# Three more heads with P·v in float32, and an earlier frozen start for two experts

## The chip, the cores and the metric

The kernel runs on one core of a Trainium2 chip. The metric is the time of one execution in microseconds (us), in the median over several. All engines of the core work at the same time, each through its own instructions in order: TensorE (matmuls; PE in rows, its weight loads PEld), VectorE (DVE), ScalarE (ACT), GpSimd (POOL) and SyncE (SP), which here only issues transfers (DMA). They wait for one another by semaphores.

## The reference

Attention over 4 batches of 8 heads, 576 positions and head size 64, with a mask by blocks of 64; its output is the input of a dense layer, and that one's output the input of a top-2 mixture of 8 experts:

```python
scores = np.where(block_i >= block_j, q @ k.T / sqrt(D), -1e9)
attn = softmax(scores); x = (attn @ v) as [2304, 512]
x = ((x @ w1) * (x @ w2)) @ w3 @ w_out            # 512 -> 1024 -> 1024 -> 512
noisy = x @ w_gate + log1p(exp(x @ w_noise)) * noise
top2, top2_w = the two largest of 8 and their softmax
out[t] += top2_w * (relu(x[t] @ w1[e]) @ w2[e])   # for both e of each token
```

## The kernel before

Products that need float32 accuracy are made of F32R halves: `split` writes a high half (a cast, on ScalarE) and a low half (source less high half, on VectorE, or on GpSimd with `low="pool"`), and `mm3` multiplies high·high, high·low and low·high in three matmuls (L470 to L472).

The attention (`attention`) takes 32 heads one after the other. Its operations stand in two strings, FIRST for the first ten steps and LATER, in which each letter is a step: `g` makes transposed probabilities `pt` of a group of columns (transposes, then a copy at L657 and a low half at L659), `a` and `b` multiply them by v (`av`, L678), `c` converts a piece of the dense layer's weights, `f` runs a stretch of that layer. The weights come as 64-bit integers' halves into `stg` by SyncE's loads, are unpacked on VectorE (`stf`, L528 to L530) and split into the pieces `pc0` to `pc11`. Heads 0 to 7 multiply P and v as plain float32 (`vz` is v with ones beside it, `pt` has one slot); heads 8 to 31 use high and low halves of P and v (`vv`, L600 and L601), in which P·v has two passes.

The dense layer (`Moe1`) runs over nine chunks of 256 tokens. `ab(c, f)` for f = 0 to 7 makes x·w1 and x·w2 of a slice (the products `m`, copied at L205, multiplied into `at` at L206, split into `gt`), `yout(c, t, part)` makes the chunk's output rows `y` (copied at L222, stored to `yt`). The router of chunk c runs in small ticks beside the next chunk; it counts the tokens of each expert (`run_cnt`) and scatters their numbers into the table `idt`. `x_load` and `x_prep` bring the attention's output into a chunk's x ahead of time (`xab`, `xr`, `xh`).

The mixture works per expert on 640 slots, five tiles of 128 rows: slots 0 to 2 (s = 0) and 3 to 4 (s = 1). `gather` fetches rows of `yt` by the table's ids, `trans` transposes and splits them (`xt`), `ffn1` makes eight `ht` slices, `ffn2(e, i)` makes an output tile `yo`, and a scatter-add puts it into the output (L933). The pieces of the experts' weights are loaded by `load_next` in order of use, 12 in memory at a time; before the dense layer has ended they go through two staging buffers, `xab` and `xr`. Expert 0's first three tiles start early: after chunk 7 has been counted, in chunk 8's last part, `freeze` fixes those slots, so that they hold tokens of counted chunks only, and `start_early` loads their ids (`ids0`) and gathers. The rest of the mixture runs in `phase3`.

Of the kernel before, what the change touches and what calls it, by code (L numbers as in the profile page):

```python
# [62 lines left out]
ZC, NF = 3, 10  # L63
PIECE_PRIO, W_PRIO, MOE_PRIO = -60, -400, -200
# [17 lines left out]
class Moe1:  # L82
# [22 lines left out]
    def setup(self):  # L105
# [13 lines left out]
        self.tr0 = p2.tile([P, E, NSLOT], I32, name="tr0")  # L119
# [8 lines left out]
    def setup_dram(self, step):  # L128
        nc, a, k = self.nc, self.a, self.k
        if step == 0:  # L130
            tab = k.idt.rearrange("(e s) o -> e (s o)", e=E)
            for dst, src in k.slots(tab, self.tr0):
                nc.sync.dma_start(dst, src)
            nc.sync.dma_start(tab[:, CAP:].rearrange("e (t c) -> t e c", c=P), self.tr1.unsqueeze(1).broadcast_to([NOV, E, P]))
            n = CH // P + 1
            dst = k.yt[NT - CH:, :].rearrange("(a p) d -> p a d", p=P)
            nc.sync.dma_start(dst[:, :, DM:], self.z[:, 0:n * E].rearrange("p (a e) -> p a e", a=n))
            for b in range(DM // CH):
                nc.sync.dma_start(dst[:, :, b * CH:(b + 1) * CH], self.z.unsqueeze(1).broadcast_to([P, n, CH]))
        else:  # L140
            n = -(-(NT // P + 1) // 4) * P
            dst = a["out"][(step - 1) * n:min(step * n, NT + P), :].rearrange("(p a) (b d) -> p (a b) d", p=P, d=CH)
            nc.sync.dma_start(dst, self.z.unsqueeze(1).broadcast_to([P, dst.shape[1], CH]))

# [49 lines left out]
    def ab(self, c, f):  # L194
# [13 lines left out]
        self.marks = (*self.k.split((gt[:, 0, :], gt[:, 1, :]), at, low="pool"), v)  # L208
# [40 lines left out]
    def router(self, c):  # L249
# [102 lines left out]
        for t in range(TPC):  # L352
            y = self.ys[c, t]
            v.tensor_tensor(y[:, DM:ROW], oh[0][:, t, :], oh[1][:, t, :], op=OP.add)
            t0 = (c * TPC + t) * P
            nc.sync.dma_start(k.yt[t0:t0 + P, :], y)
# [6 lines left out]
    def steps(self):  # L363
# [21 lines left out]
        for c in range(NCH):  # L385
# [4 lines left out]
            for f in range(8):  # L390
# [12 lines left out]
            if c == NCH - 1:  # L403
                for _ in self.rt:
                    pass
                self.freeze()
# [12 lines left out]
    def freeze(self):  # L419
# [5 lines left out]
        nc.tensor.matmul(pc[:, 0:1], self.tri[:, 1, :], cb[:, 0:1], start=True, stop=True)  # L425
        m = p2.tile([P, 1], F32, name="miss")
        v.tensor_tensor(m, self.room, pc[:, 0:1], op=OP.subtract)
        v.tensor_scalar(m, m, 0.0, float(NA), op0=OP.max, op1=OP.min)
        v.tensor_tensor(self.run_cnt[:, 0:1], self.run_cnt[:, 0:1], m, op=OP.add)
        self.k.start_early()  # L430

    def tail(self):
# [3 lines left out]
        for _ in self.rest:  # L436
            pass
        for _ in self.rt:
            pass
# [11 lines left out]
class Kernel:  # L451
    def __init__(self, tc, a):
        self.tc, self.nc, self.a = tc, tc.nc, a
        self.loaded = 0
        self.x2w = {}

# [77 lines left out]
    def attention(self):  # L534
        tc, nc, a = self.tc, self.nc, self.a
        moe1 = self.moe1
        with tc.tile_pool(name="p1", bufs=1, side="right") as p1, tc.tile_pool(name="stg", bufs=2, side="right") as self.stg, \
# [13 lines left out]
            px = pxs.enter_context(tc.tile_pool(name="px", bufs=1))  # L551
# [43 lines left out]
            def prep_v(h):  # L595
                c = hd[h]
                if h < H:
# [44 lines left out]
            def g_unit(h, g):  # L642
                c = hd[h]
                pb = pbs[h < H and h % 2]
                if g == 0:
                    if h < H:
                        c.pt = px.tile([P, 1, PTW], F32, name="pt", bufs=2)
                    else:
# [9 lines left out]
                if h >= H:  # L658
# [190 lines left out]
    def load_next(self):  # L849
# [11 lines left out]
        if self.early:  # L861
            t = self.moe1.p2b.tile([P, 1024], F32, name="xr" if n % 2 else "xab")
# [3 lines left out]
        self.split((self.pc[i][:, 0, :], self.pc[i][:, 1, :]), t)  # L866
# [4 lines left out]
    def start_early(self):  # L871
# [4 lines left out]
        self.ids0 = self.pa.tile([P, NA], I32, name="ids0")  # L876
        nc.sync.dma_start(self.ids0, self.slots(self.tab, self.ids)[0][0][:, 0, :])
        self.gather(0, 0)

    def idx(self, e, i):  # L880
        ids = self.ids0[:, i:i + 1] if e == 0 and i < NA else self.ids[:, e, i:i + 1]
# [6 lines left out]
    def gather(self, e, s):  # L888
        for i in self.part(s):
            if self.early:  # L890
                t = self.pa.tile([P, ROW], F32, name="xga", bufs=NA)
# [3 lines left out]
            self.nc.gpsimd.indirect_dma_start(out=t, out_offset=None, in_=self.yt, in_offset=self.idx(e, i))  # L895
# [13 lines left out]
    def ffn1(self, e, s):  # L909
        nc, x, n = self.nc, self.xt[e, s], len(self.part(s)) * P  # L910
        hh = self.ht[e, s] = (self.pa if s == 0 else self.pb).tile([P, 2, 8, n], F32R, name=f"ht{s}")
        for f in range(8):
# [5 lines left out]
            nc.scalar.activation(hh[:, 0, f, :], ph, AF.Relu)  # L918
            nc.vector.scalar_tensor_tensor(hh[:, 1, f, :], ph, 0.0, r32(hh[:, 0, f, :]), op0=OP.max, op1=OP.subtract)  # L919

    def ffn2(self, e, i):
# [9 lines left out]
        yo = self.pa.tile([P, DM], F32, name="yo", bufs=2)  # L931
        nc.scalar.activation(yo, po, AF.Copy, scale=self.wv[e, s][:, o:o + 1])  # L932
        nc.gpsimd.indirect_dma_start(out=self.a["out"], out_offset=self.idx(e, i), in_=yo, in_offset=None, compute_op=OP.add)  # L933

    def phase3(self):
        nc = self.nc
        with self.tc.tile_pool(name="pb", bufs=1, reuse_waits="tile") as self.pb:
            for src, dst in self.slots(self.tab, self.ids):
                nc.sync.dma_start(dst, src)
            for _ in range(4):  # L940
                self.load_next()
            self.gather(0, 1)
            self.gather(1, 0)
            self.gather(1, 1)
            for e in range(E):
                if e == 0:
                    self.trans(0, 1)
                else:
                    self.ffn1(e, 0)
                self.ffn1(e, 1)  # L950
                if e + 1 < E:
                    for s in range(2):
                        self.trans(e + 1, s)
# [4 lines left out]
                for i in range(0 if e else NA, NSLOT):  # L958
# [99 lines left out]
```

## Time and profile before

| | |
|---|---|
| median of 3 runs | 1110.45 us (1108.77 to 1111.13) |
| the profiled execution | 1110.5 us, span 1108.6 us |
| TensorE busy | 1050.8 us (95%) |
| VectorE, ScalarE, GpSimd busy | 569.8, 496.6, 310.7 us |
| TensorE's mean granted clock | 0.985 of full speed |

The span is the time from the first to the last instruction of the trace; the profiled execution's own time is 1.9 us above it. An engine's busy time counts its instructions and leaves out waits.

### The profile page before, as it was taken

What the parts mean: (1) busy time and instruction counts of PE and PEld (TensorE: products, weight loads), DVE (VectorE), ACT (ScalarE), POOL (GpSimd) and SP (SyncE); (2) the same over time, 40 slices, a digit from 0 to 9 for tenths busy, and PEclk for the clock granted to TensorE, in tenths of its full rate; (3) what the DMA queues carried; (4) which work ended last, traced back from release to release, by engine and by line L of the source; (5) the groups of instructions that cost most, each with busy time, mean ns of one, the idle gap of its engine ahead of it and who ended that gap; (6) DMA issues with size and microseconds to landing.
All of it is one profiled execution on the core that took longest, in us unless ns stands there. A gap on an engine that the chain in (4) does not pass through costs nothing.

```text
span 1108.6 us, 17533 instructions
## 1 busy us (share of the span) xinstructions
PE 1050.8 (95%) x6588; PEld 940.1 (85%) x6588; DVE 569.8 (51%) x1269; ACT 496.6 (45%) x1180; POOL 310.7 (28%) x315
## 2 busy tenths in 40 slices
PE   5989878999999999999999998999999999999996
PEld 3767776899898989989999787989898989989894
DVE  6988879866675747433346424433333342424120
ACT  5865546666666666422225324433333333333120
POOL 3110313325152342332442335241313222120202
PEclk9999989899999999999999998999999999999999
DMA  9765775335634463413433148453544445351303
GB/s 224 245 200 187 199 193 184 113 92 126 181 96 108 147 163 97 112 45 58 77 56 111 56 131 229 139 148 100 143 105 136 113 125 124 105 114 30 38 10 41
DMA packets 79442, 135.81 MB, mean 122 GB/s; under 512 B 21005, under 2 KB 45813, under 8 KB 79349
## 3 DMA queue, kind: packets, MB, share of 16 engines
q1 hardware_dynamic: 69237, 113.44, 36.0%
q0 software_dynamic: 10112, 21.16, 10.3%
q8 instruction: 54, 0.88, 0.3%
q14 instruction: 39, 0.32, 0.1%
HBM read 103.92 MB, written 30.66 MB: 121 GB/s over the span
## 4 chain that ended last, share of the span: by engine, by line
PE 78%; DMA 8%; DVE 8%; issue 2%; ACT 1%; SPq 1%; POOL 1%; POOLq 0%; DVEq 0%; ACTq 0%
PE ph L470 13%; PE ph L471 12%; PE ph L472 12%; PE m L470 9%; PE m L472 9%; PE m L471 9%; PE tp L653 4%; PE av L678 4%; DMA stg<-in_w_dram 3%; PE sb L623 2%; PE sb L620 2%; PE m L906 1%; DVE pc L465 1%; DVE nm L634 1%; DMA stf<-in_m_dram 1%
## 5 line engine op out<-in xcount | busy, mean ns | idle before, releaser
L470 PE MATMUL m<-xh,pc 128*128 128x256 f32 x576 | 165.7, 291 | 7.7 <-DVE at L206 5.5
L471 PE MATMUL m<-xh,pc 128*128 128x256 f32 x576 | 163.1, 287 | 2.6 <-DVE xh L465 2.6
L472 PE MATMUL m<-xh,pc 128*128 128x256 f32 x576 | 161.1, 286 | 1.4 <-DVE pc L465 1.4
L470 PE MATMUL ph<-xt,pc 128*128 128x256 f32 (+1 forms) x512 | 157.4, 309 | 5.2 <-ACT xt L461 5.2
L471 PE MATMUL ph<-xt,pc 128*128 128x256 f32 (+1 forms) x512 | 157.5, 308 | 0.0
L472 PE MATMUL ph<-xt,pc 128*128 128x256 f32 (+1 forms) x512 | 157.2, 307 | 0.0
L465 DVE TENSOR_TENSOR pc<-stf,pc 128x1024 fp32r<-128x1024 f32 (+1 forms) x96 | 96.4, 1018 | 104.4 <-ACT pc L461 101.1
L919 DVE SCALAR_TENSOR_TENSOR ht<-ph,ht 128x256 fp32r<-128x256 f32 (+1 forms) x128 | 61.8, 489 | 130.8 <-ACT ht L918 130.7
L470 PE MATMUL ph<-pc,ht 128*128 128x512 f32 x320 | 128.0, 401 | 0.0
L471 PE MATMUL ph<-pc,ht 128*128 128x512 f32 x320 | 126.3, 395 | 0.0
L472 PE MATMUL ph<-pc,ht 128*128 128x512 f32 x320 | 126.2, 395 | 0.0
L933 POOL DMA_INDIRECT out_dram<-yo,ids x40 | 65.1, 1626 | 199.4 <-ACT yo L932 106.6
L461 ACT CAST pc<-stf 128x1024 fp32r<-128x1024 f32 (+1 forms) x96 | 82.2, 872 | 83.8 <-DMA stf<-in_m_dram 50.1
L470 PEld LDWEIGHTS m<-xh,pc 128*128 128x128 f32 x576 | 110.3, 192 | 9.9 <-DVE at L206 6.1
L918 ACT ACTIVATE ht<-ph 128x256 fp32r<-128x256 f32 (+1 forms) x128 | 55.3, 437 | 130.7 <-PE ph L472 130.5
L465 POOL TENSOR_TENSOR gt<-at,gt 128x256 fp32r<-128x256 f32 x72 | 59.0, 823 | 194.3 <-ACT gt L461 184.6
L471 PEld LDWEIGHTS m<-xh,pc 128*128 128x128 f32 x576 | 110.0, 192 | 3.3 <-DVE xh L465 2.9
L639 ACT ACTIVATE pb<-sb,nm 128x288 f32<-128x288 f32 (+3 forms) x192 | 93.7, 497 | 41.1 <-DVE nm L637 19.3
L472 PEld LDWEIGHTS m<-xh,pc 128*128 128x128 f32 x576 | 108.8, 192 | 2.0 <-DVE pc L465 1.6
L470 PEld LDWEIGHTS ph<-xt,pc 128*128 128x128 f32 x512 | 96.6, 189 | 6.0 <-ACT xt L461 5.4
L593 POOL TENSOR_TENSOR kl<-qk,hi 128x576 fp32r<-128x576 f32 x32 | 47.8, 1493 | 179.0 <-ACT hi L591 128.1
L471 PEld LDWEIGHTS ph<-xt,pc 128*128 128x128 f32 x512 | 96.8, 189 | 0.4
(156 smaller groups left out, 2224.0 us busy)
## 6 DMA issues: line engine op xcount, KB each, us to landing
stf<-in_m_dram SPq DMA_DIRECT2D x56, 512.0 KB
qk<-in_qk_dram SPq DMA_DIRECT2D x32, 576.0 KB
stg<-in_w_dram SPq DMA_DIRECT2D x32, 512.0 KB
x<-ev SPq DMA_DIRECT2D x32, 288.0 KB
xab<-x SPq DMA_DIRECT2D x20, 256.0 KB
yt<-y SPq DMA_DIRECT2D x18, 260.0 KB
stg<-in_w_out_dram SPq DMA_DIRECT2D x8, 512.0 KB
v<-in_v_dram SPq DMA_DIRECT2D x24, 160.0 KB
```

What stands on the lines that cost most here:

```text
L461: d = nc.scalar.copy(h, src)
L465: return d, eng.tensor_tensor(l, src, r32(h), op=OP.subtract)
L470: nc.tensor.matmul(out, a, c, start=first, stop=False)
L471: nc.tensor.matmul(out, a, d, start=False, stop=False)
L472: nc.tensor.matmul(out, b, c, start=False, stop=last)
L593: nc.gpsimd.tensor_tensor(c.kl, c.qk[:, 1, :], r32(c.hi[:, 1, :]), op=OP.subtract)
L639: nc.scalar.activation(pb[t][:, k0:k0 + src.free_size()], src, AF.Exp, bias=nm, scale=1.0, accum_out=sums[:, h // H, t + n, h % H:h % H + 1])
L653: nc.tensor.transpose(bank[:, n * P:(n + 1) * P], pb[t][:, kt * P:(kt + 1) * P], self.ident)
L678: nc.tensor.matmul(c.av[:, o0:o0 + w], c.vv[:, kt, :], c.pt[:, i, s0:s0 + w], start=(kt == 0 and i == 0), stop=(kt == 4 and i == m - 1))
L918: nc.scalar.activation(hh[:, 0, f, :], ph, AF.Relu)
L919: nc.vector.scalar_tensor_tensor(hh[:, 1, f, :], ph, 0.0, r32(hh[:, 0, f, :]), op0=OP.max, op1=OP.subtract)
L933: nc.gpsimd.indirect_dma_start(out=self.a["out"], out_offset=self.idx(e, i), in_=yo, in_offset=None, compute_op=OP.add)
```

## The change

`HF = 11`: heads 8 to 10 are multiplied like heads 0 to 7, with P as copied from PSUM and v as loaded. The freeze moves from the end of chunk 8's `ab` into chunk 7 (after f = 5, behind the rest of chunk 6's router) and covers experts 0 and 1; the ids of both are loaded after the first output of chunk 7, and their rows gathered after f = 1 of chunk 8, five tiles at once, since `xga` has five buffers. Rows of chunk 7 in `yt` are zeroed beforehand too. The loads of the experts' first pieces come one by one, and a piece is converted only when two are staged and the next is to be loaded, or when `conv_next` is called. Expert 1's first three tiles go through `trans` and `ffn1` before `phase3`. The last expert makes three output tiles ahead of its second `ffn1`; the last tile's scaling is shared by ScalarE and VectorE.

```diff
+HF = 11
@@ load_v, prep_v, the copy into pt
-                if h < H:
-                    c.vv = vz[h % 2]
+                if h < HF:
+                    if h < H:
+                        c.vv = vz[h % 2]
+                    else:
+                        c.vv = p1.tile([P, 5, P], F32, name="vv")
+                        nc.gpsimd.memset(c.vv[:, :, D:], 0.0)
                     nc.sync.dma_start(c.vv[:, :, 0:D], a["v"][h])
                     return
...
-                if h >= H:
+                if h >= HF:
                     nc.vector.tensor_tensor(c.pt[:, 1, base:base + o], src, r32(h_), op=OP.subtract)
@@ Moe1.steps
-                if c == NCH - 1 and f % 2 == 1:
+                if c == NCH - 1 and (f == 1 or f > 2):
+                    if f == 1:
+                        self.k.load_next()
                     self.k.load_next()
-                    self.k.load_next()
+                if c == NCH - 2 and f == 5:
+                    for _ in self.rt:
+                        pass
+                    self.freeze()
+                if c == NCH - 1 and f == 1:
+                    with self.tc.issue_after(self.marks[1].ins):
+                        self.k.gather(0, 0)
+                        self.k.gather(1, 0)
...
+                    if c == NCH - 2 and (t, part) == (0, 0):
+                        self.k.start_early()
+                    elif c == NCH - 1 and (t, part) == (0, 0):
+                        self.k.load_next()
+                    elif c == NCH - 1 and (t, part) in ((0, 1), (1, 0)):
+                        self.k.conv_next()
@@ run
                     for i in range(NA):
                         self.ffn2(0, i)
+                    self.trans(1, 0)
+                    self.ffn1(1, 0)
                     self.moe1.p2s.close()
@@ load_next
         if self.early:
+            if len(self.staged) == 2:
+                self.conv_next()
             t = self.moe1.p2b.tile([P, 1024], F32, name="xr" if n % 2 else "xab")
...
         nc.sync.dma_start(t, src)
-        self.split((self.pc[i][:, 0, :], self.pc[i][:, 1, :]), t)
+        self.staged.append((i, t))
+        if not self.early:
+            self.conv_next()
+
+    def conv_next(self):
+
+        if self.staged:
+            i, t = self.staged.pop(0)
+            with ExitStack() as es:
+                for m in self.marks if self.early else ():
+                    es.enter_context(self.tc.issue_after(m.ins))
+                self.split((self.pc[i][:, 0, :], self.pc[i][:, 1, :]), t)
@@ phase3
-                else:
+                elif e > 1:
                     self.ffn1(e, 0)
+                if e == E - 1:
+                    for i in range(NA):
+                        self.ffn2(e, i)
                 self.ffn1(e, 1)
```

In the rows that follow, a tile's number behind the underscore tells one use of a name from another, and line numbers are those of the kernel in question (the changed one's are higher).

VectorE in the attention, while head 9 is under way, before (`pt` is the low half of P, `stf` and `pc` a piece of the dense layer's weights, `nm` a maximum for the softmax):

```order
L465 TENSOR_TENSOR pc4_71<-stf_1078,pc4_71 128x512
L634 TENSOR_REDUCE nm2_1608<-sb_1604 128x1
L659 TENSOR_TENSOR pt_1559<-tp_1560,pt_1559 128x448
L530 SCALAR_TENSOR_TENSOR stf_1106<-stg_1074,stf_1106 128x512
L659 TENSOR_TENSOR pt_1559<-tp_1567,pt_1559 128x448
L634 TENSOR_REDUCE nm3_1615<-sb_1611 128x1
L465 TENSOR_TENSOR pc4_71<-stf_1106,pc4_71 128x512
L528 TENSOR_SCALAR stf_1114<-stg_1082 128x512
L206 TENSOR_TENSOR at_1653<-at_1653,m_1628 128x256
L206 TENSOR_TENSOR at_1692<-at_1692,m_1667 128x256
L529 SCALAR_TENSOR_TENSOR stf_1114<-stg_1082,stf_1114 128x512
L659 TENSOR_TENSOR pt_1559<-tp_1576,pt_1559 128x512
```

and with the change:

```order
L553 TENSOR_SCALAR stf_1114<-stg_1082 128x512
L663 TENSOR_REDUCE nm0_1580<-sb_1574 128x1
L663 TENSOR_REDUCE nm1_1582<-sb_1574 128x1
L663 TENSOR_REDUCE nm2_1590<-sb_1586 128x1
L554 SCALAR_TENSOR_TENSOR stf_1114<-stg_1082,stf_1114 128x512
L488 TENSOR_TENSOR pc4_71<-stf_1106,pc4_71 128x512
L213 TENSOR_TENSOR at_1634<-at_1634,m_1609 128x256
L663 TENSOR_REDUCE nm3_1597<-sb_1593 128x1
L555 SCALAR_TENSOR_TENSOR stf_1114<-stg_1082,stf_1114 128x512
L488 TENSOR_TENSOR pc5_72<-stf_1114,pc5_72 128x512
```

The subtractions into `pt` are gone, and the unpacking of `stg_1082` stands ahead of the product `at`.

SyncE at the same place, before (`stg` is a piece of weights, `xab` and `xr` the second chunk's x, `qk` and `v` the next heads'):

```order
L162 DMA xab_1659<-x2_61 64x4x256
L574 DMA qk_1557<-in_qk_dram 128x1152
L162 DMA xab_1659<-x2_61 64x4x256 x2
L519 DMA stg_1082<-in_w2_dram 128x2x256
L167 DMA xr_1660<-rs_62 64x4x256 x2
L583 DMA v_1730<-in_v_dram 128x320
L519 DMA stg_1110<-in_w2_dram 128x2x256
L519 DMA stg_1118<-in_w1_dram 128x2x256
```

and with the change:

```order
L609 DMA vv_1543<-in_v_dram 128x5x64
L544 DMA stg_1082<-in_w2_dram 128x2x256
L713 DMA x2_61<-ev_1512 128x576
L169 DMA xab_1640<-x2_61 64x4x256 x2
L599 DMA qk_1546<-in_qk_dram 128x1152
L169 DMA xab_1640<-x2_61 64x4x256
L174 DMA xr_1641<-rs_62 64x4x256
L169 DMA xab_1640<-x2_61 64x4x256
L544 DMA stg_1110<-in_w2_dram 128x2x256
```

The load of `stg_1082` now goes ahead of the second chunk's x.

ScalarE at the end of chunk 8, before (`pc` are casts of expert 0's pieces from the staging buffers `xab` and `xr`, `y` the two output copies of the chunk):

```order
L205 COPY at_7372<-m_7347 128x256
L461 CAST gt_7375<-at_7372 128x256
L461 CAST pc2_69<-xab_7422 128x1024
L461 CAST pc3_70<-xr_7426 128x1024
L205 COPY at_7409<-m_7384 128x256
L461 CAST gt_7412<-at_7409 128x256
L222 COPY y_7472<-m_7447 128x512
L222 COPY y_7499<-m_7474 128x512
L461 CAST yT_7506<-m_7501 128x4x128
```

and with the change:

```order
L484 CAST pc5_72<-xr_7279 128x1024
L212 COPY at_7395<-m_7370 128x256
L484 CAST gt_7398<-at_7395 128x256
L484 CAST pc0_67<-xab_7327 128x1024
L484 CAST pc1_68<-xr_7368 128x1024
L484 CAST pc2_69<-xab_7410 128x1024
L229 COPY y_7441<-m_7412 128x512
L484 CAST pc3_70<-xr_7427 128x1024
L229 COPY y_7472<-m_7445 128x512
L484 CAST yT_7483<-m_7478 128x4x128
L484 CAST xt0_7587<-m_7590 128x4x128
```

Six pieces are cast behind the last `at` copies in place of two, and the second `y` copy stands behind the cast of the last of them, `pc3`.

ScalarE around expert 0's early tiles, before (`ht` is expert 0's or 1's first layer, `yo` an output tile, `xt` the transposed rows of the next):

```order
L461 CAST pc8_75<-stf_7848 128x1024
L932 ACTIVATE yo_7782<-ph_7757,wv0_7611 128x512
L461 CAST pc9_76<-stf_7852 128x1024
L461 CAST pc10_77<-stf_7856 128x1024
L932 ACTIVATE yo_7810<-ph_7785,wv0_7611 128x512
L461 CAST pc11_78<-stf_7860 128x1024
L461 CAST xt1_7878<-m_7881 128x4x128
L461 CAST xt1_7878<-m_7889 128x4x128
L461 CAST xt0_8017<-m_8020 128x4x128
L932 ACTIVATE yo_7838<-ph_7813,wv0_7611 128x512
L918 ACTIVATE ht1_7896<-ph_7897 128x256
```

and with the change:

```order
L963 ACTIVATE ht0_7613<-ph_7727 128x384
L484 CAST xt0_7830<-m_7833 128x4x128
L987 ACTIVATE yo_7767<-ph_7742,wv0_7588 128x512
L484 CAST pc10_77<-xab_7676 128x1024
L987 ACTIVATE yo_7797<-ph_7772,wv0_7588 128x512
L484 CAST pc11_78<-xr_7710 128x1024
L987 ACTIVATE yo_7827<-ph_7802,wv0_7588 128x512
L484 CAST xt0_7830<-m_7841 128x4x128
L484 CAST xt0_7830<-m_7849 128x4x128
L963 ACTIVATE ht0_7856<-ph_7857 128x384
L963 ACTIVATE ht0_7856<-ph_7872 128x384
```

Pieces 8 to 11 come from the staging buffers, one at a time between expert 0's tiles, and expert 1's `ht` in 384 columns follows at once.

## Rows read from the trace of the kernel before

**Rows 1.** The page: busy us, share of the span and instructions of each engine.
```profile
...
PE 1050.8 (95%) x6588; PEld 940.1 (85%) x6588; DVE 569.8 (51%) x1269; ACT 496.6 (45%) x1180; POOL 310.7 (28%) x315
...
```

**Rows 2.** Stretches: engines' busy us (instructions), granted clock, DMA share, GB/s.
```profile
...
150.00:200.00 50.00, 38.02 (x243) 33.33 (x244) 45.16 (x82) 29.84 (x81) 16.01 (x13) 0.89 0.58 177
160.00:170.00 10.00, 8.69 (x65) 7.48 (x64) 9.94 (x21) 7.86 (x23) 2.77 (x2) 1.00 0.69 232
210.00:220.00 10.00, 10.00 (x62) 8.61 (x61) 6.35 (x12) 6.50 (x19) 5.18 (x4) 1.00 0.44 129
...
```

**Rows 3.** Chain of waits from 115 to 175 us: start, us, what.
```profile
...
121.03 0.53 DVE pt L659
...
146.19 11.70 DMA stg<-in_w_dram
...
172.81 0.47 DVE pt L659
...
```

**Rows 4.** Waits of VectorE from 100 to 215 us: total, times, longest.
```profile
...
DVE stf L528 <- DMA stg<-in_w_dram: 11.9, 6, 6.2
...
```

**Rows 5.** TensorE in order of time: start, us, operation [idle before <-releaser].
```profile
...
154.80 0.58 PE L470 MATMUL m<-xh,pc 128*128 128x256 f32 x1 [5.32 <-DVE at L206]
...
606.94 0.18 PE L425 MATMUL m<-cb,tri 128*128 128x1 bf16 x1 [1.04 <-DVE cb L423]
...
622.46 0.66 PE L229 MATMUL m<-ident,y 128*128 128x128 f32 x4 [0.45 <-ACT y L222]
624.02 0.66 PE L906 MATMUL m<-ident,xga 128*128 128x128 f32 x4 [0.91 <-DMA xga<-yt,ids]
624.51 0.60 PE L229 MATMUL m<-ident,y 128*128 128x128 f32 x4
...
628.32 0.96 PE L470 MATMUL ph<-xt,pc 128*128 128x384 f32 x4
...
669.28 1.01 PE L470 MATMUL ph<-xt,pc 128*128 128x256 f32 x3 [5.18 <-ACT xt L461]
...
```

**Rows 6.** ScalarE in order of time.
```profile
...
587.67 1.05 ACT L461 CAST pc<-xab 128x1024 fp32r<-128x1024 f32 x1 [0.82 <-PE m L471]
...
612.05 1.05 ACT L461 CAST pc<-xr 128x1024 fp32r<-128x1024 f32 x1 [1.80 <-DMA xr<-in_m_dram]
...
621.82 1.07 ACT L222 COPY y<-m 128x512 f32<-128x512 f32 x2 [6.23 <-PE m L472]
...
667.21 1.04 ACT L461 CAST pc<-stf 128x1024 fp32r<-128x1024 f32 x1 [4.21 <-DMA stf<-in_m_dram]
...
1092.74 0.69 ACT L932 ACTIVATE yo<-ph,wv 128x512 f32<-128x512 f32 x1 [4.91 <-PE ph L472]
...
```

**Rows 7.** Two stretches at the seam between the MoEs.
```profile
...
622.46:628.45 5.99, 3.96 (x29) 3.25 (x30) 2.83 (x5) 3.27 (x6) 1.91 (x5) 1.00 0.45 126
669.28:674.00 4.72, 4.72 (x24) 4.55 (x25) 2.12 (x4) 0.59 (x1) 2.58 (x8) 0.57 1.03 315
...
```

**Rows 8.** GpSimd in order of time, at the end.
```profile
...
1094.93 1.55 POOL L933 DMA_INDIRECT out_dram<-yo,ids  x1 [3.90 <-DMA out_dram<-yo,ids]
1100.44 1.55 POOL L933 DMA_INDIRECT out_dram<-yo,ids  x1 [3.97 <-DMA out_dram<-yo,ids]
```

**Rows 9.** Groups by shape, VectorE: busy us, mean ns, idle before.
```profile
...
L659 DVE TENSOR_TENSOR pt<-tp,pt 128x448 fp32r<-128x448 f32 x48 | 28.6, 616 | 11.7 <-ACT pt L657 11.7
...
L659 DVE TENSOR_TENSOR pt<-tp,pt 128x512 fp32r<-128x512 f32 x24 | 16.5, 687 | 13.7 <-ACT pt L657 13.6
...
L659 DVE TENSOR_TENSOR pt<-tp,pt 128x384 fp32r<-128x384 f32 x24 | 13.2, 551 | 5.9 <-ACT pt L657 5.9
...
```

**Rows 10.** Groups by shape, TensorE.
```profile
...
L678 PE MATMUL av<-pt,vv 128*128 128x448 f32 x96 | 33.5, 405 | 0.0
...
L678 PE MATMUL av<-pt,vz 128*128 128x448 f32 x32 | 15.1, 555 | 0.0
...
```

More of the change, by code (lines that the diff above doesn't have):

```diff
@@ L134, in setup_dram @@
             nc.sync.dma_start(tab[:, CAP:].rearrange("e (t c) -> t e c", c=P), self.tr1.unsqueeze(1).broadcast_to([NOV, E, P]))
[L135 to L139, printed above, removed]
-        else:
+            self.y_zeros(NT - CH, CH // P + 1)
+        else:
+            if step == 1:
+                self.y_zeros(NT - 2 * CH, CH // P)
             n = -(-(NT // P + 1) // 4) * P
@@ L143, in setup_dram, with y_zeros @@
             nc.sync.dma_start(dst, self.z.unsqueeze(1).broadcast_to([P, dst.shape[1], CH]))
+    def y_zeros(self, r, n):
+        dst = self.k.yt[r:r + n * P, :].rearrange("(a p) d -> p a d", p=P)
+        self.nc.sync.dma_start(dst[:, :, DM:], self.z[:, 0:n * E].rearrange("p (a e) -> p a e", a=n))
+        for b in range(DM // CH):
+            self.nc.sync.dma_start(dst[:, :, b * CH:(b + 1) * CH], self.z.unsqueeze(1).broadcast_to([P, n, CH]))
     @staticmethod
@@ L207, in ab @@
         gt = self.gts[c, f] = self.p2b.tile([P, 2, CH], F32R, name="gt", bufs=8)
-        self.marks = (*self.k.split((gt[:, 0, :], gt[:, 1, :]), at, low="pool"), v)
+        self.marks = self.k.marks = (*self.k.split((gt[:, 0, :], gt[:, 1, :]), at, low="pool"), v)
     def yout(self, c, t, part):
@@ L355, in router @@
             t0 = (c * TPC + t) * P
-            nc.sync.dma_start(k.yt[t0:t0 + P, :], y)
+            d = nc.sync.dma_start(k.yt[t0:t0 + P, :], y)
+            for j in k.early_gathers:
+                tc.declare_no_dep(d.ins, j.ins, reason="frozen slots have tokens of routed chunks only")
         yield
@@ L402, in steps @@
             ahead(c + 1)
[L403 to L406, printed above, removed]
             for t in range(TPC):
@@ L437, in tail @@
             pass
+        for _ in range(2):
+            k.load_next()
         for _ in self.rt:
@@ L454, in __init__ @@
         self.loaded = 0
+        self.staged, self.marks = [], ()
         self.x2w = {}
+        self.early_gathers = []
     def split(self, dst, src, act="act", low="dve"):
@@ L647, in g_unit @@
                         c.pt = px.tile([P, 1, PTW], F32, name="pt", bufs=2)
+                    elif h < HF:
+                        c.pt = p1.tile([P, 2, PTW], F32, name="pt")[:, 0:1, :]
                     else:
@@ L894, in gather @@
             self.xg[e, i] = t
-            self.nc.gpsimd.indirect_dma_start(out=t, out_offset=None, in_=self.yt, in_offset=self.idx(e, i))
+            d = self.nc.gpsimd.indirect_dma_start(out=t, out_offset=None, in_=self.yt, in_offset=self.idx(e, i))
+            if e < 2 and s == 0:
+                self.early_gathers.append(d)
     def trans(self, e, s):
@@ L930, in ffn2 @@
                      (wt[:, 0, c:c + 512], wt[:, 1, c:c + 512]), f == 0, f == 7)
-        yo = self.pa.tile([P, DM], F32, name="yo", bufs=2)
-        nc.scalar.activation(yo, po, AF.Copy, scale=self.wv[e, s][:, o:o + 1])
+        yo = self.pa.tile([P, DM], F32, name="yo", bufs=3)
+        wv = self.wv[e, s][:, o:o + 1]
+        if e == E - 1 and i == NSLOT - 1:
+            h = DM // 2
+            nc.scalar.activation(yo[:, 0:h], po[:, 0:h], AF.Copy, scale=wv)
+            nc.vector.tensor_scalar(yo[:, h:], po[:, h:], wv, None, op0=OP.mult)
+        else:
+            d = nc.scalar.activation(yo, po, AF.Copy, scale=wv)
+            if self.early and e == 0 and self.staged:
+                self.marks = (d,)
+                self.conv_next()
         nc.gpsimd.indirect_dma_start(out=self.a["out"], out_offset=self.idx(e, i), in_=yo, in_offset=None, compute_op=OP.add)
@@ L957, in phase3 @@
                     self.load_next()
-                for i in range(0 if e else NA, NSLOT):
+                for i in range(0 if 0 < e < E - 1 else NA, NSLOT):
                     self.ffn2(e, i)
```

39 lines of the change are left out of this document (19 added, 20 removed).

## The prediction

> **What bounds the kernel now.** I read the busy times first: TensorE has work for 95% of the span, no other engine for more than 51% [rows 1]. A gain can therefore come only from the few places where TensorE waits or runs at half clock, and work added to it costs in full wherever it does not wait. The table of stretches gives the places [rows 2]: from 150 to 200 us TensorE is busy 38.0 of 50 us at a mean clock of 0.89; VectorE is full there (9.94 of 10 us in 160 to 170), and from 210 on TensorE is full (10.00 of 10). So in the attention's middle VectorE sets the pace. The rest is at the seam between the two MoEs and after the last matmul.
>
> The chain of waits shows what VectorE's pace is made of [rows 3]: nine subtractions of P's low part for heads 8 to 10 stand in it, the first at 121.03 and the last at 172.81 (4.5 us in all), but also transfers of staged weights, the longest 11.70 us; by VectorE's table of waits it stands 11.9 us for them between 100 and 215 [rows 4]. TensorE in order of time shows that from the other side: at 154.80 it had stood 5.32 us for an `at` product [rows 5], which is queued on VectorE behind the conversion of a weight piece that had not arrived.
>
> At the seam the same view [rows 5] has a 1.04 us wait at the freeze, 0.45 and 0.91 us between the last y transposes and the first gathered rows, and the first matmul of expert 0 at 628.32. The largest wait of the second half follows at 669.28: 5.18 us for `xt`, which ScalarE converts only behind the cast at 667.21 that had waited 4.21 us for a piece of expert 1's weights [rows 5, 6]. Then the clock is 0.57 for 4.7 us [rows 7].
>
> At the end two scatter-adds each wait about 4 us for the one before [rows 8].
>
> **The change, part by part.** The sum is made against the profiled execution, 1110.5 us for a span of 1108.6; the median of the three runs, 1110.45, is the same number.
>
> *Heads 8 to 10.* Gone are per head two subtractions of 616 ns, one of 687 and one of 551 [rows 9], together 2.47 us, 7.4 us for three heads; also three casts on ScalarE and three subtractions on GpSimd, neither of them full there. Added are three fills on GpSimd and a slower P·v on TensorE. 448 columns take 555 ns in float32 against 405 [rows 10], so 0.33 ns more a column; a head has four such matmuls and two each of 320, 192 and 128 columns, 3072 columns, which makes 1.0 us a head and 3.1 in all. These lie in the 12 us that TensorE waits between 150 and 200 [rows 2]; without that cover they would cost all 3.1. What VectorE gives back is at least nothing (if the staged transfers take up every us) and at most 7.4. The 4.5 us that stand in the chain are the nearest row; part of it will turn into waits for transfers, part of the 5.32 us goes as well, because the order puts the load of that piece (stg_1082) ahead of the loads of the second x chunk. I take **−4**, bounds +1 (if TensorE's waits don't cover a third of P·v's 3.1) and −7.4. From 210 on TensorE is the bound, so whatever is won before stays won.
>
> *The other attention edits* (three more zero stores, one tile in another pool): nothing. No row of the zeros stands in the chain, and the DMA engines are busy 0.58 of that stretch [rows 2]. If they push a staged load, that is within the bound of +1.
>
> *The seam, start.* The freeze now falls in chunk 7 and the gathers land during chunk 8, so 1.04 us and the wait for gathered rows go. But expert 0's eight pieces start later. Before, the first is cast at 587.67, as soon as it may, and the eighth at 612.05 [rows 6]. Now two loads are held, and the first cast comes only when the third load is issued, after f=3 of chunk 8, about 11 us later. Two staging buffers carry eight pieces in turn, so 24.4 us from first cast to last stay about the same: 612.05 + 11 to 12 = 623 to 624 for the eighth. In ScalarE's order the second y copy stands behind that cast, so it runs at about 624.8 instead of 622.4, its transposes at 625.4 instead of 624.5. From there to the first matmul of expert 0 took 3.8 us (624.5 to 628.3); I take the same less a little: **+0.7** (−1.5, if the pieces come sooner, so that only the vanished waits count, to +2.5, if the rounds of loads take longer; the eighth cast already waited 1.80 us for its load [rows 6]). TensorE now stands some 2.5 us, from 622.9, where it stood 0.45. Whether it drops the clock lies between two rows: after the short waits here it was 1.00, after 5.18 us it was 0.57 for 4.7 us, which cost 4.7 × 0.43 = 2.0 [rows 7]. I take **+2**, nearer to the long one as the transposes around it are sparse; at best 0.
>
> The Trainium skill ("TensorE: Matmul & The Clock Gate", HAM oscillation) says that gaps in TensorE's work bring the clock down, so that the work behind them starts cold; the row at 669.28 agrees (0.57). By that rule the 2 us stay in and the sum is 1102; by the row at 622.46 (1.00 across waits of 0.45 and 0.91) they drop out and it is 1100.
>
> *The seam, end.* Expert 1's first 384 rows are multiplied before the pieces and rows that 669.28 waited for are needed. The stall of 5.18 and its half clock of 2.0 go; what stays are two joints (before expert 1's early and late rows), where a transpose and its conversion precede the first use: 0.7 each by what two copies of that size on ScalarE take, 1.07 us for both, and as much for the start [rows 6]. Pieces 10 and 11 are converted behind the first two output tiles of expert 0, one tile ahead of use, and the rest that 669.28 waited for arrives while these 384 rows run. **−7.2 + 1.4 = −5.8**; bounds −7.2 and −2 (if one joint waits 5 us).
>
> *The end.* The last scatter waits for the one before, which waited too: 1094.93, then 1100.44, 5.5 us apart [rows 8]. With three tiles of the last expert done before ffn1(7,1), the fourth goes right after its copy (1092.74 + 0.69 + 0.3 = 1093.7 [rows 6]), the fifth at 1093.7 + 5.5 = 1099.2 in place of 1100.44: **−1.2**, with 0 as the bound if the landing stays longer. The copy in halves makes that possible, it adds nothing of its own.
>
> Sum: −4 + 0.7 + 2 − 5.8 − 1.2 = −8.3, so **1102.2 us**, taken as 1102.
>
> **The rivals.**
> *Transfers set the attention's pace.* For it: 11.70 us for one staged piece in the chain [rows 3]. Against: after 160 VectorE is full and its loads are issued as it frees their buffers, so its own time is in the loop. Then the first term is 0: 1106. The Trainium skill ("DMA: Bandwidth & Descriptors", Issuing engines are not separate DMA queues) says that transfers of all issuing engines share the same DMA engines; it speaks for this rival, as the added zeros and the early gathers would then lengthen staged loads. The row above fits either reading.
>
> *The reordered loads give more.* The 5.32 us go with their half clock [rows 5], and the subtractions bring more than those in the chain: the first term is about −11 (the 12 us idle from 150 to 200 are the limit), 1095. For it: both loads stand earlier in the new order; against: VectorE was full after 160, and TensorE pays the 3.1 us.
>
> *The seam gives nothing back.* Each round of staged loads takes over a us longer because the gathers and the y stores run beside them; the y copy comes at 627, the gap grows to 5 us like that at 664, and the next clock rise takes another 2 us. First part +2.5 and +4, second −5.8: the seam is +0.7, the time 1105.5 to 1107, and with half of the attention's gain 1108 to 1109.
>
> *Slower: the second x chunk comes late.* Its loads now stand behind one more staged piece, and the products of the second chunk wait for them on TensorE, with everything behind them in its order. The price is one staged transfer, 5.3 to 11.7 us [rows 3, 5], and 2 of half clock; at the upper end, less the 4 us of relief, the first term is +9.7 and the time 1110.5 + 9.7 − 4.3 = 1115.9. It decides from 6.5 us on (the 4.3 of the other terms and 2.2). For it: VectorE's 11.9 us of waits for staged pieces show that this queue is full at that time [rows 4]; against: the chunk's x is needed only after the first chunk's eight parts, which are not all done.
>
> **How the numbers follow.** Forecast 0.41 (own range 1098.5 to 1105); transfers in the attention 0.17 (1106); more from the loads 0.15 (1095); the seam without gain 0.15 (1107 to 1109); slower 0.12 (1116). The forecast's bounds on the single terms go with the rivals; 1095 to 1110 leaves out the slower case and half of the best: some 0.8. A difference of 0.2%, 2.2 us, is about what a measurement of this kernel can tell from none. Faster: 0.41 + 0.17 + 0.15, and nearly half of the fourth, 0.79; same 0.09; slower 0.12.
>
> **What the profile after would show.** No VectorE subtraction into `pt` before head 11; TensorE's idle in 150 to 200 well under 12 us, and the wait of 5.32 gone or moved. The freeze's matmul without a row of its own in the chain near 600. The second y copy behind a cast at 623 to 625, and the first matmul of expert 0 at 628 to 631 after allowing for the shift from the attention. No wait over 2 us between that and expert 1's late rows, with the clock at 1.00. The last two scatters 5.5 us apart and the last within 1 us of the copy. The forecast is wrong if TensorE's idle before 210 stays above 15 us, or if a new wait at the seam exceeds 4 us.

## The result, and the profile after

The changed kernel takes 1115.59 us (median of 13 runs, 1112.51 to 1119.71), beside 1109.89 for the kernel before on the same chip; the ratio is 1.0052, interval 1.004 to 1.0065. It is slower by about 5.7 us, where I had forecast 8 us faster. The profiled execution has a span of 1115.4 us.

To see where the time went I follow five places through the traces: the last y copy of chunk 7 (its start on ScalarE), the first matmul of expert 0, the second output tile of expert 3, the last matmul, and the span.

| us | y copy, chunk 7 | first expert matmul | tile of expert 3 | last matmul | span |
|---|---|---|---|---|---|
| before | 582.81 | 628.32 | 852.32 | 1097.77 | 1108.6 |
| changed | 589.92 | 638.90 | 859.18 | 1105.01 | 1115.4 |
| difference | +7.1 | +10.6 | +6.9 | +7.2 | +6.8 |

So by these marks the loss is all made before 590 us, where the attention and the dense layer run; the seam loses 3.5 us more and gives 3.7 back, and the end does nothing. TensorE in order of time, with what it waited for before the row, beside [rows 5] (`xh` are the F32R halves of a chunk's x, `tp` a bank of a head's transposes, `sb` a head's scores, `hi` the high halves of q and k that make them):

```profile
...
140.06 0.38 PE L493 MATMUL m<-xh,pc 128*128 128x256 f32 x1 [4.49 <-ACT xh L484]
144.35 0.58 PE L494 MATMUL m<-xh,pc 128*128 128x256 f32 x1 [3.37 <-DVE xh L488]
...
175.27 0.39 PE L493 MATMUL m<-xh,pc 128*128 128x256 f32 x1 [1.30 <-DVE at L213]
...
269.99 0.55 PE L684 MATMUL tp<-ident,pb 128*128 128x128 f32 x3 [4.23 <-DVE ev L699]
...
383.57 0.55 PE L684 MATMUL tp<-ident,pb 128*128 128x128 f32 x3 [1.67 <-DVE ev L699]
385.08 0.33 PE L649 MATMUL sb<-hi 128*128 128x192 f32 x1 [0.96 <-DVE hi L619]
...
630.45 1.11 PE L236 MATMUL m<-ident,y 128*128 128x128 f32 x4 [3.67 <-ACT y L229]
...
633.68 1.11 PE L236 MATMUL m<-ident,y 128*128 128x128 f32 x4 [1.27 <-ACT y L229]
...
638.90 1.03 PE L493 MATMUL ph<-xt,pc 128*128 128x384 f32 x4
...
675.58 0.97 PE L493 MATMUL ph<-xt,pc 128*128 128x384 f32 x4 [0.86 <-ACT xt L484]
...
694.24 0.74 PE L493 MATMUL ph<-xt,pc 128*128 128x256 f32 x4 [0.73 <-ACT xt L484]
...
724.88 0.39 PE L493 MATMUL ph<-xt,pc 128*128 128x256 f32 x1 [1.10 <-DVE ht L964]
...
```

The 5.32 us for `at` have become 1.30, but the two waits for the first chunk's x have grown to 4.49 and 3.37. In the kernel before they were:

```profile
...
133.85 0.38 PE L470 MATMUL m<-xh,pc 128*128 128x256 f32 x1 [1.44 <-ACT xh L461]
...
137.60 0.58 PE L471 MATMUL m<-xh,pc 128*128 128x256 f32 x1 [2.64 <-DVE xh L465]
...
```

The large new wait stands where no row of before had one: 4.23 us at 269.99. Stretches with engines' busy times and TensorE's granted clock, beside [rows 2, 7]:

```profile
...
100.00:150.00 50.00, 41.78 (x210) 33.36 (x209) 39.69 (x75) 24.68 (x63) 6.78 (x5) 0.91 0.68 183
150.00:200.00 50.00, 42.19 (x293) 37.43 (x292) 40.81 (x78) 29.23 (x81) 16.13 (x13) 0.96 0.68 189
...
265.70:270.00 4.30, 0.07 (x2) 0.01 (x1) 0.35 (x2) 0.00 (x0) 0.46 (x1) 1.00 0.30 72
270.00:274.60 4.60, 4.60 (x16) 3.70 (x17) 1.63 (x4) 2.53 (x8) 1.85 (x3) 0.63 0.71 203
...
629.00:634.30 5.30, 2.59 (x11) 2.19 (x12) 2.35 (x2) 3.60 (x6) 0.99 (x1) 0.50 0.51 172
634.30:640.00 5.70, 5.70 (x29) 5.43 (x27) 3.35 (x6) 2.42 (x5) 0.18 (x1) 0.58 0.44 144
...
```

and the first of them in the kernel before:

```profile
...
100.00:150.00 50.00, 45.06 (x255) 37.73 (x253) 43.74 (x83) 27.84 (x74) 8.34 (x5) 0.97 0.73 192
...
```

TensorE's idle time from 150 to 200 us has fallen from 12.0 to 7.8 us, but from 100 to 150 it has grown from 4.9 to 8.2. Behind the 4.23 us the clock is 0.63 for 4.6 us, which costs 1.7 more. The chain of waits from 250 to 300 us (start, us, what) says whom TensorE waited for:

```profile
...
254.12 9.68 DMA yt<-y
...
263.82 5.65 DMA rs<-ev
...
269.65 0.30 DVE ev L699
...
269.99 0.55 PE tp L684 x3
...
```

SyncE's issues at that place, in order of time:

```profile
...
253.75 0.86 SPq L363 DMA_DIRECT2D yt<-y  x2
257.95 1.24 SPq L169 DMA_DIRECT2D xab<-x  x2
259.54 0.68 SPq L612 DMA_DIRECT2D v<-in_v_dram  x1
260.31 3.77 SPq L724 DMA_DIRECT2D rs<-ev  x5
268.94 1.24 SPq L174 DMA_DIRECT2D xr<-rs  x2
...
```

and the same in the kernel before:

```profile
...
248.97 1.25 SPq L162 DMA_DIRECT2D xab<-x  x2
252.00 1.65 SPq L693 DMA_DIRECT2D rs<-ev  x5
253.75 1.24 SPq L167 DMA_DIRECT2D xr<-rs  x2
259.96 1.15 SPq L356 DMA_DIRECT2D yt<-y  x2
...
```

`rs` are the reciprocal row sums of the second batch of eight heads: five small stores from a buffer named `ev`, which the next heads use for their output. Before, they went out ahead of the two y stores of the dense layer; now they stand behind these, a chunk's x and a head's v. Until they have been read, VectorE cannot copy the next head's result into `ev`, and TensorE's next transposes wait for that. The table of the tile `ev`, who was waited for (us, times), names 10.4 us where before no row has such a wait:

```profile
...
  DMA rs<-ev: 10.4, 2
...
```

The place in the queue is not the whole of it. The sums themselves are made later, on VectorE in the changed kernel:

```profile
...
258.56 0.94 DVE L721 RECIPROCAL ev<-ev 40x128 f32<-40x128 f32 x1
...
```

and in the kernel before:

```profile
...
251.02 0.94 DVE L690 RECIPROCAL ev<-ev 40x128 f32<-40x128 f32 x1
...
```

They are ready at 259.50 where they were at 251.96, and the first store goes out 0.8 us after that. What the y stores hold up is the last of the five: SyncE's table of waits from 240 to 275 us (total, times, longest) has 2.2 us for a y store to land before an issue of row sums,

```profile
...
SPq L724 <- DMA yt<-y: 2.2, 1, 2.2
...
```

and in the chain above the last store then takes 5.65 us.

At the seam ScalarE, beside [rows 6]:

```profile
...
605.17 1.04 ACT L484 CAST pc<-xab 128x1024 fp32r<-128x1024 f32 x1
...
628.86 1.04 ACT L484 CAST pc<-xab 128x1024 fp32r<-128x1024 f32 x1 [3.13 <-DMA xab<-in_m_dram]
629.81 0.58 ACT L229 COPY y<-m 128x512 f32<-128x512 f32 x1
...
632.10 1.04 ACT L484 CAST pc<-xr 128x1024 fp32r<-128x1024 f32 x1 [1.70 <-DMA xr<-in_m_dram]
633.05 0.58 ACT L229 COPY y<-m 128x512 f32<-128x512 f32 x1
...
```

Both y copies come only when a cast ahead of them has got its load. At the end GpSimd, beside [rows 8]:

```profile
...
1101.17 1.54 POOL L991 DMA_INDIRECT out_dram<-yo,ids  x1 [14.08 <-ACT yo L987]
1106.85 1.54 POOL L991 DMA_INDIRECT out_dram<-yo,ids  x1 [4.13 <-DVE yo L985]
```

### The profile page after: what moved, and what is told of

It is laid out like the page before. It is cut to its first block, busy times and chain, and to the rows that moved or that the text cites. A ratio compares the mean times of both kernels' runs of the same rounds, so it can differ in the third digit from the quotient of the medians.

```text
span 1115.4 us, 17476 instructions
## 1 busy us (share of the span) xinstructions
PE 1053.0 (94%) x6588; PEld 944.6 (85%) x6588; DVE 558.3 (50%) x1258; ACT 494.2 (44%) x1177; POOL 310.5 (28%) x315
## 3 DMA queue, kind: packets, MB, share of 16 engines
q0 software_dynamic: 10112, 21.16, 10.4%
## 4 chain that ended last, share of the span: by engine, by line
PE 77%; DMA 11%; DVE 8%; ACT 1%; issue 1%; SPq 1%; POOL 0%; POOLq 0%; DVEq 0%; ACTq 0%
PE ph L493 13%; PE ph L494 13%; PE ph L495 13%; PE m L493 8%; PE m L495 8%; PE m L494 8%; DMA stg<-in_w_dram 5%; PE tp L684 3%; PE av L709 3%; PE sb L652 2%; PE sb L649 2%; PE m L951 1%; DVE pc L488 1%; DVE stf L555 1%; DMA stg<-in_w_out_dram 1%
## 5 line engine op out<-in xcount | busy, mean ns | idle before, releaser
L493 PE MATMUL ph<-xt,pc 128*128 128x384 f32 (+1 forms) x512 | 156.3, 308 | 2.7 <-ACT xt L484 1.6
L494 PE MATMUL ph<-xt,pc 128*128 128x384 f32 (+1 forms) x512 | 157.2, 307 | 0.0
L495 PE MATMUL ph<-xt,pc 128*128 128x384 f32 (+1 forms) x512 | 156.9, 307 | 0.0
L964 DVE SCALAR_TENSOR_TENSOR ht<-ph,ht 128x384 fp32r<-128x384 f32 (+1 forms) x128 | 62.0, 490 | 149.6 <-ACT ht L963 149.6
L488 DVE TENSOR_TENSOR pc<-stf,pc 128x1024 fp32r<-128x1024 f32 (+1 forms) x92 | 90.8, 1001 | 91.1 <-ACT pc L484 88.4
L963 ACT ACTIVATE ht<-ph 128x384 fp32r<-128x384 f32 (+1 forms) x128 | 55.1, 437 | 137.1 <-PE ph L495 137.1
L484 ACT CAST pc<-stf 128x1024 fp32r<-128x1024 f32 (+1 forms) x92 | 78.0, 863 | 69.9 <-DMA stf<-in_m_dram 30.8
```

The costliest lines, as they stand in the source:

```text
L484: d = nc.scalar.copy(h, src)
L488: return d, eng.tensor_tensor(l, src, r32(h), op=OP.subtract)
L493: nc.tensor.matmul(out, a, c, start=first, stop=False)
L494: nc.tensor.matmul(out, a, d, start=False, stop=False)
L495: nc.tensor.matmul(out, b, c, start=False, stop=last)
L963: a = nc.scalar.activation(hh[:, 0, f, :], ph, AF.Relu)
```

## The experiments

My theory after the result: the three heads cost the time, and not by their own work, but because they shift the order that the instructions are put in, so that the row-sum stores stand late on SyncE. The rivals: float32 P·v costs TensorE the time, or the extra zero stores lengthen the transfers. The seam is asked for by itself. Ratios are to the kernel before on the same chip.

**Heads 8 to 10 as before, the rest as changed.**

```diff
-HF = 11
+HF = 8
```

> The changed kernel with HF = 8, so that heads 8 to 10 keep their high and low halves; all else as changed. Theory (the three heads' new cost in the instruction order: the dense chunk runs ahead, and the row-sum stores of the second batch stand on SyncE behind y stores and x loads, so that the next use of ev waits 4.2 us at 270 and 1.7 us at 384): the last y copy of chunk 7 is back at about 582.8 us (before: 582.81, changed: 589.92), no wait over 1 us between 215 and 600, and the time is 1109 to 1110.5, because the seam gives about 0 and the end 0.4. Rival 1 (float32 P times v itself costs TensorE the time, 3 us): 1112 to 1113, as the other 3 to 4 us would stay. Rival 2 (the three extra zero stores lengthen the transfers): nothing comes back, 1115 to 1117, chunk 7 at 589.

Measured: 1108.13 us, ratio 0.9966 (0.9948 to 0.9983); chunk 7's y copy at 581.83, the waits for `ev` gone, and SyncE issues the row sums (251.17) ahead of the y stores (259.15) again. TensorE's waits from 215 to 600 us (total, times, longest) begin with:

```profile
...
PE m L245 <- ACT yT L484: 1.1, 2, 0.7
PE m L236 <- DVE at L213: 0.5, 1, 0.5
...
```

So the whole loss is in the heads, 0.86% or 9.5 us (1.0052 against 0.9966). The zero stores, which are still in this kernel, cost nothing that can be measured. What is left of the change is faster than before by 3.8 us (1.9 to 5.8 by the interval).

**Only the heads.** The lines of the diff with `HF`, put into the kernel before:

```diff
+HF = 11
...
-                if h < H:
+                if h < HF:
...
-                if h >= H:
+                if h >= HF:
```

> The kernel before with HF = 11 alone, nothing else. Theory (order of SyncE's stores): chunk 7's last y copy at 588 to 591, the wait for ev near 270 of about 4 us is there, time 1116 to 1118, about 7 us above before. Rival 1 (P times v only): about 3 us above before, 1113, and no wait near 270. Rival 2 (zero stores, which are not in this kernel): 1106 to 1110.

Measured: 1121.92 us, ratio 1.0081 (1.0052 to 1.0111); y copy at 590.42, and among TensorE's waits from 215 to 600:

```profile
...
PE tp L661 <- DVE ev L676: 6.0, 2, 5.3
...
```

It is the same wait, 6.0 us in all, 5.9 (4.23 and 1.67) in the changed kernel, and here too SyncE issues the row sums (261.11) behind the y stores (254.07). 0.81% is 9.0 us: too much for the 3.1 that the prediction reckoned for float32 P·v.

**The row sums in a tile of their own.** Order, heads and stores as in the changed kernel; only the buffer is another:

```diff
-                st = p1.tile([40, P], F32, name="ev")
+                st = p1.tile([40, P], F32, name="st")
```

> The changed kernel, with the reciprocal row sums in a tile of their own instead of the buffer named ev, so that the next head's ev copy no longer waits for the five row-sum stores; order of the stores unchanged. Theory: the waits near 270 (4.2 us and about 1.7 of half clock) and near 384 (1.7 and 1.0) go, chunk 7's last y copy at about 582 to 584, time 1108 to 1110. Rival 1 (P times v on TensorE): the waits go, but another one takes their place, since TensorE's work is the limit: time 1113 to 1116. Half of it each: 1111 to 1112.

Measured: 1109.06 us, ratio 0.9968 (0.995 to 0.9986). The stores still stand behind the y stores, and their issue takes 4.58 us, but TensorE and VectorE no longer wait for them:

```profile
...
257.11 0.87 SPq L363 DMA_DIRECT2D yt<-y  x2
...
263.78 4.58 SPq L724 DMA_DIRECT2D rs<-st  x5
...
```

0.84%, 9.3 us, come back. By time this is the kernel with HF = 8 again. Its y copy at 586.02 is later than expected. The profiled execution was the slowest of the twelve (1114.15, 5 us above the median), and it was behind the changed kernel's already ahead of these stores: by 1.1 us at 72.78, where the same matmul stood at 71.64, and by 3.4 at chunk 0's first y copy (219.05 against 215.68).

**That tile with HF = 8**, as a control (both edits above).

> HF = 8 and the row sums in their own tile: the control for the two runs above and for the tile of its own. With the old order of the stores no wait for ev exists, so the theory expects no difference from HF = 8 alone: chunk 7's last y copy at 581 to 583, time 1107 to 1109. If the tile of its own helps in itself (the rival to the order of the stores), 577 to 579 and 1103 to 1105.

Measured: 1108.73 us, ratio 0.9969 (0.9956 to 0.9982), y copy at 582.12. The tile helps only where the stores are late; and with it, heads 8 to 10 in float32 or in halves make no difference that can be measured (0.9968 and 0.9969, to 0.0018 and 0.0013 either way).

**The two last pieces of expert 0 after the y copies.** Pieces 6 and 7 are needed only after expert 0's first layer:

```diff
-                if c == NCH - 1 and (f == 1 or f > 2):
+                if c == NCH - 1 and (f == 1 or 2 < f < 7):
...
-                    elif c == NCH - 1 and (t, part) == (0, 0):
-                        self.k.load_next()
-                    elif c == NCH - 1 and (t, part) in ((0, 1), (1, 0)):
-                        self.k.conv_next()
...
-            if self.early and e == 0 and f in (3, 5):
+            if self.early and e == 0 and f % 2 == 0:
```

> The changed kernel, with pieces 6 and 7 of expert 0 (second layer, needed only after ffn1 of expert 0) loaded and converted after chunk 8's y copies, the later ones in step with f = 0, 2, 4, 6 of that ffn1. Theory for the seam (the two y copies stand on ScalarE behind casts that wait for their loads: 3.67 and 1.27 us of TensorE and half clock for about 5 us): these waits go, the first matmul of expert 0 comes 5 to 7 us sooner against chunk 7's y copy than in the changed kernel (48.98 us there), time 1109 to 1111. Rival (the staging chain only moves: casts that wait for loads now hold up ht copies in expert 0's first ffn1): a new wait of 2 us or more in 630 to 660, time 1113 to 1116.

Measured: 1111.58 us, ratio 0.999 (0.997 to 1.001): 0.62%, 6.9 us, better than the changed kernel. From chunk 7's y copy to the first matmul of expert 0 it takes 41.96 us (592.70 to 634.66), where the changed kernel takes 48.98 and the one before 45.51. No single wait of TensorE over 1.5 us follows up to 760 us.

**Both repairs without the heads**: HF = 8 and the late pieces.

> Heads 8 to 10 as before (HF = 8) and the two last pieces of expert 0 after chunk 8's y copies, all else as changed. Theory (the two losses found so far add up: about 8 us for the heads, about 7 for the casts ahead of the y copies): chunk 7's last y copy at 582, the first matmul of expert 0 about 42 us later (624), time 1100 to 1103, 7 to 9 us below before. Rival (the seam's gain is eaten by a later wait, since pieces arrive later): 1105 to 1108.

Measured: 1103.05 us, ratio 0.9915 (0.9895 to 0.9935). TensorE in order of time at the seam, where the two y copies (618.53) now stand ahead of the two late casts:

```profile
...
619.17 0.66 PE L236 MATMUL m<-ident,y 128*128 128x128 f32 x4 [0.45 <-ACT y L229]
620.09 0.60 PE L236 MATMUL m<-ident,y 128*128 128x128 f32 x4
621.47 0.39 PE L245 MATMUL m<-yT,wcat 128*128 128x256 f32 x1 [0.34 <-ACT yT L480]
623.70 0.95 PE L489 MATMUL ph<-xt,pc 128*128 128x384 f32 x4
...
```

and the stretch of it, with the clock at 1.00:

```profile
...
617.00:624.00 7.00, 6.21 (x42) 5.01 (x41) 4.40 (x6) 4.81 (x9) 0.99 (x1) 1.00 0.62 181
...
```

**Both repairs with the heads**: HF = 11, own tile, late pieces.

> The changed kernel with both repairs (row sums in their own tile, the two last pieces after the y copies), heads 8 to 10 in float32 as changed. If the remaining 4 us of the heads are theirs whatever comes later: chunk 7's last y copy at 585 to 586, first matmul of expert 0 about 42 us later, time 1106 to 1108, some 4 us above the same kernel with HF = 8 (1103). If they were a matter of the order of that one run: 1102 to 1104.

Measured: 1102.7 us, ratio 0.9909 (0.9886 to 0.9932): the same as with HF = 8. It is the changed kernel less two waits, and beats it by 1.4% and the kernel before by 0.9%. The time is that of the second reading; the y copy, at 585.26, is that of the first, in a profile that is again the slowest of its runs (1105.07, of six).

**What float32 and VectorE's relief are worth apart.** First, float32 P·v without the relief: the twelve subtractions are still made, their result is not used.

```diff
+                elif h >= H:
+                    nc.vector.tensor_tensor(c.pl[:, 1, base:base + o], src, h_, op=OP.subtract)
```

> The changed kernel with the row sums in their own tile, and with the twelve subtractions of heads 8 to 10 still made on VectorE (their result is not used). So float32 P times v is paid and VectorE is not relieved. If the relief is worth 4 us: chunk 7's last y copy at 590, 4 us after the 586.0 with the relief; if it is worth nothing: 585 to 587 again, and the 4 us above HF = 8 are the price of P times v and of the other order. Time 1112 to 1114 and 1108 to 1110.

Measured: 1115.98 us, ratio 1.0042 (1.0026 to 1.0057), 0.74% or 8.2 us above the same with the relief, and 0.73% above HF = 8 with the same tile (0.9969). That is as much as the subtractions take in all (7.4 us; the intervals leave 5.6 to 10.9), and this kernel has waits of its own for VectorE (3.6 us for `pt`, 3.2 for `hi`).

Second, the relief without float32: P's low half of heads 8 to 10 is left out (F32R, one pass).

```diff
-                    elif h < HF:
-                        c.pt = p1.tile([P, 2, PTW], F32, name="pt")[:, 0:1, :]
+                    elif h < HP:
+                        c.pt = p1.tile([P, 2, PTW], F32R, name="pt")[:, 0:1, :]
```

> HF = 8, row sums in their own tile, and heads 8 to 10 leave out P's low half: P times v is one pass with F32R v, and the twelve subtractions on VectorE are gone. So VectorE is relieved as in the change, and TensorE by 2 to 3 us a head instead of burdened. If VectorE's relief is worth its 4 us there (the prediction's term): chunk 7's last y copy at 574 to 578, 4 to 8 us before the 581.8 of HF = 8; if other waits (the first chunk's x, staged pieces) take it up: 580 to 584 in spite of less work. Time 1100 to 1104 and 1106 to 1110.

Measured: 1108.19 us, ratio 0.9951 (0.9932 to 0.9969), y copy at 579.58: 0.18% or 2 us below the control, which the intervals can't tell from nothing, though both VectorE and TensorE have less to do. The two readings of the relief, 8 and 2 us, don't agree.

Third, six heads in float32 (`HF = 14`) with the own tile.

> Six heads (8 to 13) instead of three in float32, row sums in their own tile. If float32 P times v costs TensorE 1.0 us a head and more, with little relief from VectorE: chunk 7's last y copy 3 to 5 us after the 586.0 of three heads, 589 to 591, time 1113 to 1115. If the first three heads' 4 us come from the order of transfers around the first x chunks, and further heads cost nothing: 585 to 587, 1109 to 1111. If VectorE's relief is worth its 2.5 us a head where it is full (160 to 210): below 584.

Measured: 1111.09 us, ratio 0.9983 (0.9965 to 1.0002), y copy at 583.20. Against three heads (0.9968) that is no clear difference: 1.7 us more, give or take 2.9, so a price of 1 us a head is neither seen nor excluded. The y copy is below 584, as the reading by VectorE's relief had it, but 1.1 us after that of HF = 8 (582.12): against heads in halves nothing is won here either.

## Why the prediction was wrong, point by point

**The heads, −4 forecast, +9.5 measured.** The step that failed is the sentence "From 210 on TensorE is the bound, so whatever is won before stays won". TensorE was the bound there in the order that stood; the heads moved the order. The dense layer ran 6 us ahead of its old time (first y copy of chunk 0 at 215.68, before 221.91) and the attention 7.5 us behind (the second batch's sums at 259.50, before 251.96), while TensorE had been busy no longer (180.19 us up to 215.7, before 180.50): nothing had been won. The dense layer's stores now stood ahead of the row sums in SyncE's queue, and the one buffer `ev` tied TensorE to them: 4.23 and 1.67 us of waits, 1.7 of half clock, 0.96 behind the second, 8.6 together. Undoing the heads, giving the row sums a tile and putting the heads alone into the old kernel each move the time by 9 to 9.5 us (shown). Why these heads make the scheduler choose that order is not shown. I had compared the queue's order at 140 us, where I knew of a wait, and not where it meets the second batch.

Of the prediction's signs of being wrong one came, if the idle time is counted from 100 us: up to 210 it is 16.6 us, before 17.3, so above the 15 named. It tells that nothing was won, but not of the loss that follows. The other did not come: the new wait at the seam is 3.67, under 4.

**The heads' own work.** Without that wait the sum of P·v's price and VectorE's relief is nothing measurable (0.9968 with, 0.9969 without; 0.9909 and 0.9915 after the seam's repair), not −4. The term was mis-sized. The `at` wait shrank as forecast, 5.32 to 1.30, but the waits for the first chunk's x grew by 3.8 (7.86 less 4.08), and VectorE stood 15.3 us for staged pieces from 100 to 215 instead of 11.9 [rows 4]:

```profile
...
DVE stf L553 <- DMA stg<-in_w_dram: 15.3, 9, 3.6
...
```

This fits the rival in which transfers set the attention's pace and the term is 0, but does not show it: with the twelve subtractions put back the kernel takes 8.2 us more. The chain before had more for that rival than the prediction told: beside the 11.70 us, two transfers of staged pieces of 5.06 (at 115.45) and 5.30 us (at 125.05), against 4.5 for all nine subtractions. How much of relief and price there is singly stays open: the runs that split them have other orders, and their readings differ.

**The rival slower than before** had the right kind, a transfer late in SyncE's queue, but the wrong place: the second chunk's x cost no such wait. That its 1115.9 lies so near the measured 1115.59 is luck: its +9.7 was the price of a late staged piece, 11.70 us and 2 of half clock less 4 of relief, and the 9.5 measured are those of the row sums.

**The zero stores, nothing:** right (chunk 7's y copy at 581.83 with them and HF = 8, 582.81 before).

**The seam's start, +2.7 forecast, +3.5 measured** (48.98 less 45.51). The mechanism was right: the first cast at 605.17, the second y copy behind the eighth at 632.10, and half clock behind the gap (0.50 and 0.58). Its sizes were too small: from first cast to eighth it takes 26.9 us, not 24.4, and the two stretches at half clock cost about 2.59 × 0.50 + 5.70 × 0.42 = 3.7 us, where the sum had 2. I had overlooked that the first y copy waits as well, behind the seventh cast, which is where the larger wait is, 3.67. The Trainium skill ("TensorE: Matmul & The Clock Gate", HAM oscillation) had it that work behind such gaps starts cold: it did here, at 1.2 of 2.4 GHz, and did not across waits of 0.45 and 0.34 in the repaired kernel (1.00). The late pieces give back 7 us of this step, more than its loss against before, since the waits for the gathered rows (0.91 us at 624.02, then 0.47 and 0.65, of which the prediction names the first) and for the freeze (1.04) stay away too.

**The seam's end, −5.8 forecast, −3.7 measured** (859.18 less 638.90 is 220.28, before 224.00). The stall of 5.18 is gone, the joints cost 0.86 and 0.73, the clock holds. The joints were to cost 1.4 and cost 1.6. New is 1.10 at 724.88, for `ht` behind casts of weights on ScalarE. Another 0.8 lies in TensorE's busy time of this stretch (217.59 us, before 218.82 with 2.0 of half clock in it), not in a wait; I cannot name its cause.

**The end, −1.2 forecast, about 0 measured.** The last scatter comes 1.27 us after the last copy's start, before 2.10, as the two are no longer tied; but from its issue to the span's end it takes 8.55 instead of 8.16, and the matmuls from the tile of expert 3 to the last take 245.83 instead of 245.45.

Seam and end together were forecast at −4.3, and with the old heads they measured −3.8 by time (−1.9 to −5.8). The traces don't show where that comes from: the parts by the marks, +3.5, −3.7 and 0, make −0.2, and the span with the old heads is 1.0 us shorter than before, in one execution of runs from 1105.68 to 1111.48. So this part of the prediction holds by time, and its single terms, 0.8 to 2.1 us off, do not.

## What to carry to other kernels

An edit that moves work between engines also moves the order in which a scheduler puts the instructions, and the price can fall due 100 us later in another queue: compare the order of each queue at every place where a buffer with a single copy is reused, not only where a wait is known. A small store that shares a buffer with a hot tile is worth a tile of its own: here that was worth 9.3 us where the stores were late, and cost nothing measurable where they were not. And a conversion that waits for a load should not stand in an engine's order ahead of a copy that the critical engine waits for, when its own result is needed 29 us later (the eighth cast at 632.10, the first matmul with its piece at 661.08).

## What the hardware showed

Five stores of 2 to 4 KB took 3.77 us to issue and the last landed 5.65 us after its turn behind two 260 KB stores and a chunk's x; before, the same five were issued in 1.65. TensorE's clock was 0.50 in a stretch in which it was busy 2.59 of 5.30 us, and 0.63 after a wait of 4.23, but 1.00 across waits under half a microsecond. It need not have fallen by the end of a wait: with the old heads the same y copy made TensorE stand 3.78 us, the clock was 1.00 for 0.7 us behind it (622.80 to 623.50), and 0.51 after that. Single executions of one and the same kernel spread by 4 to 12 us here (the kernel before on two chips), so one profile can mislead by more than the effects looked for: the run with the tile of its own was profiled in its slowest execution.
